# First head pair projected by seven products between the last gate/up chunks; row sums, down-weight sums, score pairs and final adds moved

## The chip, the cores and the metric

The kernel runs on one core of a Trainium2 chip. TensorE (PE) multiplies matrices into PSUM, VectorE (DVE), ScalarE (ACT) and GpSimd (POOL) work element by element, SyncE (SP) issues the transfers. Each engine works its own queue in order and waits on semaphores. The metric is the device time of one execution in microseconds; lower is better.

## The reference

```python
def _A_ref(x, k_cache, v_cache, wq, wo):            # H = 32 heads, Dh = 128, 2048 rows, D = 512
    q = transpose((x @ wq).reshape(B, Sq, H, Dh))
    scores = einsum("bhqd,bhkd->bhqk", q, k_cache) * (Dh ** -0.5)
    p = softmax(scores)
    return transpose(einsum("bhqk,bhkd->bhqd", p, v_cache)).reshape(B, Sq, H * Dh) @ wo

def _B_ref(x, W_gate, W_up, W_down):                # F = 1792
    gate, up = x @ W_gate, x @ W_up
    return (gate * (gate > 0) * up) @ W_down

xn = layernorm(x)
out = x + _A_ref(xn, k_cache, v_cache, wq, wo) * silu(_B_ref(xn, W_gate, W_up, W_down))
```

All inputs are bf16.

## The kernel before, in words

**Rows and blocks.** The 2048 rows are four blocks Q = 0 to 3 of 512 rows. A *chunk* is 128 of the 1792 gate/up columns (14 chunks, `fc`). Attention runs over 128 blocks b = (head h, Q), each of eight *key pairs* p (two times 128 keys). For a key pair TensorE makes two score matmuls (L1258), ScalarE one exponential of 128x1024 (L1270), and three pairs later (`LAG = 3`) TensorE makes eight P·V matmuls (L1367). At a block's end VectorE normalizes (L1287, L1290), and a transfer transposes the result into `OT_store`.

**Seven products.** Where four products of half-sized blocks would make a matrix product, this kernel often makes seven (Strassen's scheme as Winograd arranged it), from sums of the operands prepared ahead: `TX` (sums of the normalized rows, `emit_tx`), `SW` (sums of a head pair's Q weights, `emit_sw`), `SG` (gate/up weights, `gu_sums`), `WdT`/`Wd16` (down weights, `emit_wd_sums`), `HS_sb` (sums of h, `emit_hs`). `emit_st(pr, c, step)` makes the projection of head pair `pr` for the row halves c and c + 2 in four steps (products 1 and 2; 6 and 5; 7 and 3; 4) and combines them on VectorE with the accumulators `cu`, `cv`. `emit_d(Q, step)` does the same for the down projection of 512 rows; step 1 needs the seventh sum of h (`hs_tok[(Q, 1, 2)]`). Only pair 0 is projected plainly, by `emit_qp`: four matmuls for each head and row block.

**The PSUM ring.** Six banks `ps_r` are three slots of two banks. `ring_acquire` hands them out in turn, and TensorE waits there until the slot's former content was read. A gate/up chunk takes one, a score pair takes one, and `emit_M` puts extra work (a step of `emit_st`, `emit_d`, `emit_os`, two final tiles) into one.

**Order of the work.** The head centres the first 512 rows and runs their gate/up and down projection on TensorE; meanwhile VectorE computes the layer norm's statistics in `ln_task(i)`, one call for each chunk, GpSimd applies them (L409), and SP transposes the rows into `xnT` (L521). The first 512 rows are normalized last, and their transposes stand on SP's queue behind `issue_first` (the first K, Q-weight, V and output-weight loads) and in front of `gu_load(0)` and `gu_load(1)`. Then `emit_gate_up(2)` runs 14 chunks for Q = 2 (L656, L660); behind its chunks VectorE makes the down-weight scale (chunks 0, 1) and sums (2 to 5), the first half of the row sums (6 to 9) and half of the sums of h (10, 11), and ScalarE and GpSimd prepare two chunks of gate/up weights (`gu_sums`, behind chunks 4 and 6). After it come the plain projections of head 0 and three score pairs, and then the main loop. Its extra work is laid down by block and key pair: `plan` holds what goes into ring slots (`at(b, p, ...)`), `side` holds VectorE work put behind it, and `defer(n, ...)` postpones by n key pairs. In the main loop an iteration emits the score pair three ahead, its plan items, its side items, its deferred work, and the P·V of its own pair. The gate/up rows Q = 1 and 3 run by seven products inside blocks 2 to 13.

**The tail.** `emit_base` scales a 128-row tile of the accumulated result and adds the input (L1235, L1240; `base_at`), where `LB` is block 124. `emit_final_tile(n)` multiplies the last four heads' part (L1401); VectorE scales it by the gate into `fin_tmp` (L1409), GpSimd adds it to the base (L1425; VectorE for the last tile), and SP stores it (L1430).

The lines around the start of the main loop read:

```python
        for Q in range(0, QB, 2):
            emit_M([(emit_qp, 1, 0, Q), (emit_qp, 1, 0, Q + 1)])
        sp_head_start(0)
        for gp in range(LAG):
            open_S_pair(gp)
            emit_S_tile(gp, 0)
            emit_S_tile(gp, 1)
        emit_sw(1)
```

Of the kernel before, what the change touches and what calls it, by code (L numbers as in the profile page):

```python
# [52 lines left out]
def bass_recurrent_scan__mha_block_cached__glu_gated_reglu__prompt_kernel(  # L53
# [30 lines left out]
    LAG = 3  # L84
# [31 lines left out]
    with ExitStack() as es:  # L116
# [70 lines left out]
        cu = at_(92160, [128, NQ], F32, "cu")  # L187
        cv = at_(94208, [128, NQ], F32, "cv")
# [336 lines left out]
        def ln_task(i):  # L525
            if i < 4 * (QB - 1):
                ln_hold["st"] = ln_stats(4 + i)
                if i % 4 == 3:
                    ns = list(range(i + 1, i + 5))
                    ln_hold["sq"] = (ns, ln_sqrt(ns, ln_aggr(ns, ln_hold["st"])))  # L530
                elif i >= 4 and i % 4 == 0:
                    ln_finish(i // 4)
            elif i == 4 * (QB - 1):
                ln_finish(QB - 1)
                issue_first()
                ns = list(range(4))
                ln_hold["sq"] = (ns, ln_sqrt(ns, sem_ln2.cur()))
            elif i == 4 * (QB - 1) + 1:
                ctok = ln_finish(0)
                _wait(dve, ctok)  # L540
                rtok = sem_ln3.sig(
                    dve.scalar_tensor_tensor(r2[:], rstd[:, 0:4, :], YSC, rstd[:, 0:4, :],
                                             op0=ALU.mult, op1=ALU.mult))
                _wait(dve, rtok)
                ln_hold["r2"] = sem_ln3.sig(
                    dve.tensor_scalar(r2h[:], r2[:], 0.5 / YSC, None, op0=ALU.mult))
# [38 lines left out]
        def gu_sums(k):  # L585
# [13 lines left out]
            gu_tok[(k, "x")] = sem_sg.sig(pool.tensor_tensor(X[:, 3], a12, X[:, 1], ALU.subtract))  # L599

# [84 lines left out]
        def emit_wd_sums(k):  # L685
            DH = D // 2
            b11, b12 = Wd_sb[:, 0:HF, 0:DH], Wd_sb[:, 0:HF, DH:D]
            b21, b22 = Wd_sb[:, HF:FC, 0:DH], Wd_sb[:, HF:FC, DH:D]
            if k == 0:
                _wait_all(dve, [wd_tok[0], wd_tok[1], sem_nm.cur()])  # L690
            elif k != 2:
                _wait(dve, wd_tok["k"])
            if k == 0:
                t = dve.tensor_tensor(WdT[:, 0], b12, b11, ALU.subtract)
            elif k == 1:
                t = dve.tensor_tensor(WdT[:, 1], b22, WdT[:, 0], ALU.subtract)
            elif k == 2:
                t = dve.tensor_tensor(Wd16[:, 0:HF, DH:D], b22, b12, ALU.subtract)
            else:
                t = dve.tensor_tensor(WdT[:, 2], WdT[:, 1], b21, ALU.subtract)  # L700
            t = sem_wdt.sig(t)
            if k != 2:
                wd_tok["k"] = t
            wd_tok["t"] = t
# [68 lines left out]
        _wait(sp, sem_g.cur())  # L773
        gu_load(0)
        gu_load(1)
        hlast = emit_gate_up(2)

        qt_ready = {}
        qp_done_tok = {}
# [28 lines left out]
        def emit_qp(h, Q, bank):  # L808
            qs = slice(Q * NQ, (Q + 1) * NQ)
            _wait(pe, wq_tok(0))  # L810
            if h == 0 and Q == 0:
                _wait_all(pe, xt_ready[0])
            ins = None
            for c in range(DC):
                ins = pe.matmul(ps_r[:, bank, :], Wq_sb[0][:, c, h, :], xnT[:, c, qs],  # L815
                                start=(c == 0), stop=(c == DC - 1))
            qtok = sem_qp.sig(ins)
            if h == 1 and Q == QB - 1:
                qp_done_tok[0] = qtok
            dst = qt_take(h, Q)  # L820
            if h == 0 and Q % 2 == 1:
                _wait(act, qtok)
                etok = sem_gua.sig(act.copy(dst, ps_r[:, bank, :]))
            else:
                _wait(dve, qtok)
                etok = sem_qpe.sig(dve.tensor_copy(dst, ps_r[:, bank, :]))
            qt_ready[(h, Q)] = etok
            return etok

        sw_tok = {}  # L830

        def emit_sw(pr):
            b = pr % 2
            W = Wq_sb[b]
            _wait(pool, wq_tok(pr))
            if pr >= 3:
                _wait(pool, qp_done_tok[pr - 2])
            wflat = W[:].rearrange("p c i e -> p (c i e)")
            if pr == 2:
                _wait(act, wq_tok(pr))  # L840
                k = sem_w2s.sig(act.activation(wflat, wflat, ACTF.Copy, scale=WSC))
            else:
                k = sem_sw.sig(pool.tensor_scalar(wflat, wflat, WSC, None, op0=ALU.mult))  # L843
            sw_tok[(pr, 0)] = k
            _wait(pool, k)
            a11, a12 = W[:, 0:HC, 0, :], W[:, HC:DC, 0, :]
            a21, a22 = W[:, 0:HC, 1, :], W[:, HC:DC, 1, :]
            X = SW[b]
            if pr == 1:
                _wait(pool, glu_done_tok)  # L850
            k1 = sem_sw.sig(pool.tensor_tensor(X[:, 0], a21, a22, ALU.add))
            sem_sw.sig(pool.tensor_tensor(X[:, 2], a11, a21, ALU.subtract))
            _wait(pool, k1)
            k2 = sem_sw.sig(pool.tensor_tensor(X[:, 1], X[:, 0], a11, ALU.subtract))
            _wait(pool, k2)
            sw_tok[(pr, 1)] = sem_sw.sig(pool.tensor_tensor(X[:, 3], a12, X[:, 1], ALU.subtract))

        st_tok = {}

        def emit_st(pr, c, step, *banks):  # L860
            W, X = Wq_sb[pr % 2], SW[pr % 2]
# [120 lines left out]
        def emit_d(Q, step, *banks):  # L982
# [271 lines left out]
        def emit_S_tile(gp, tt):  # L1254
# [8 lines left out]
            if p == NP - 1:  # L1263
                qt_free.append((qt_slot[(h, Q)], stok))
                if Q == QB - 1:
# [5 lines left out]
                               scale=scale if h < 2 else scale / WSC)  # L1271
# [119 lines left out]
        def emit_final_tile(n, bank):  # L1391
# [12 lines left out]
            fb = fin_cnt[0] % NFT  # L1404
            fin_cnt[0] += 1
            _wait(dve, otok)
            _wait(dve, fin_free[fb])
            mtok = sem_opa.sig(
                dve.scalar_tensor_tensor(fin_tmp[fb], ps_r[:, bank, 0:D], 1.0 / (OSC * YSC), g_sb[:, n, :],  # L1409
                                         op0=ALU.mult, op1=ALU.mult))  # L1410
            fin_pending.append((n, fb, mtok))
            flush_final_add()
            return mtok

        fin_pending = []

        def flush_final_add():
            if not fin_pending:
                return
            n, fb, mtok = fin_pending.pop()  # L1420
            Q, j = divmod(n, 4)
            eng, sem = (dve, sem_opa) if n == NT - 1 else (pool, sem_hp)
            _wait(eng, mtok)
            _wait(eng, base_done[n])
            ftok = sem.sig(eng.tensor_tensor(g_sb[:, n, :], s_acc[:, n, :], fin_tmp[fb], ALU.add))  # L1425
            fin_free[fb] = ftok
            if Q == QB - 1 or j % 2 == 1:
                n0 = n if Q == QB - 1 else n - 1
                _wait(sp, ftok)
                sem_out.sig(sp.dma_start(out_t[:, n0:n + 1, :], g_sb[:, n0:n + 1, :]))  # L1430

# [5 lines left out]
        at(0, 0, (emit_qp, 1, 1, 0), (emit_qp, 1, 1, 1))  # L1437
        at(1, 0, (emit_qp, 1, 1, 2), (emit_qp, 1, 1, 3))
# [22 lines left out]
        dplan = {2: ((0, 2), (0, 5), (1, 2), (1, 5)),  # L1461
# [36 lines left out]
        base_at += [(LB + 1, 6), (LB + 1, 7), (LB + 2, 2), (LB + 2, 6)]  # L1498
# [7 lines left out]

        glu_done_tok = hlast
# [65 lines left out]
        flush_final_add()  # L1573
# [29 lines left out]
```

## Time and profile before

| | us |
|---|---|
| median of 3 runs | 1256.17 |
| lowest and highest | 1255.91, 1256.29 |
| the profiled execution: time | 1255.73 |
| the profiled execution: span of its instructions | 1254.1 |
| ScalarE's exponentials (1024 of them), busy | 969.9 |
| P·V matmuls, busy | 749.2 |
| score matmuls, busy | 652.7 |

The profile is that of one execution. A row of a timeline reads: start in us from the span's start, duration, engine, line, operation, output<-inputs, tile sizes, count, and in brackets the idle time before it and what ended it. "PE" is a matmul, "PEld" a weight load, "SPq" an issue on SyncE's queue. Consecutive instructions of one form are merged into a row. The recorded end of a matmul lies about 0.17 behind the start of the next, so durations of matmuls are read from start to start.

### The profile page before, as it was taken

What the parts mean: (1) busy time and instruction counts of PE and PEld (TensorE: products, weight loads), DVE (VectorE), ACT (ScalarE), POOL (GpSimd) and SP (SyncE); (2) the same over time, 40 slices, a digit from 0 to 9 for tenths busy, and PEclk for the clock granted to TensorE, in tenths of its full rate; (3) what the DMA queues carried; (4) which work ended last, traced back from release to release, by engine and by line L of the source; (5) the groups of instructions that cost most, each with busy time, mean ns of one, the idle gap of its engine ahead of it and who ended that gap; (6) DMA issues with size and microseconds to landing.
All of it is one profiled execution on the core that took longest, in us unless ns stands there. A gap on an engine that the chain in (4) does not pass through costs nothing.

```text
span 1254.1 us, 28671 instructions
## 1 busy us (share of the span) xinstructions
PE 1234.5 (98%) x12173; PEld 868.8 (69%) x12399; DVE 681.7 (54%) x1157; ACT 1020.3 (81%) x1108; POOL 290.3 (23%) x261
## 2 busy tenths in 40 slices
PE   9999999999999999999999999999999999999998
PEld 5466565777777777777777777777777777777774
DVE  6667777665444545454543544454544444446766
ACT  4357877668888888888888888888888888888894
POOL 2323999510401040100401040102200040100005
PEclk9999999999999999999999999999999999999999
DMA  9712431332223332443222232433333222343212
GB/s 273 155 31 31 78 79 27 51 48 34 48 44 56 69 60 47 60 68 56 52 41 44 57 56 52 60 64 60 51 56 68 50 34 42 60 81 68 67 33 76
DMA packets 250687, 78.02 MB, mean 62 GB/s; under 512 B 226241, under 2 KB 250561, under 8 KB 250561
## 3 DMA queue, kind: packets, MB, share of 16 engines
q1 hardware_dynamic: 249888, 75.79, 32.6%
q8 instruction: 98, 1.61, 0.6%
q10 hardware_dynamic: 672, 0.39, 0.1%
q14 instruction: 29, 0.23, 0.1%
HBM read 38.54 MB, written 2.10 MB: 32 GB/s over the span
## 4 chain that ended last, share of the span: by engine, by line
PE 84%; ACT 10%; POOL 2%; issue 1%; SPq 1%; DVE 1%; DMA 0%; POOLq 0%; DVEq 0%; ACTq 0%
PE ps_acc L1367 34%; PE ps_r L1258 28%; ACT PT L1270 10%; PE ps_r L1139 6%; PE ps_r L879 6%; PE ps_r L943 3%; PE ps_r L1002 3%; PE ps_r L656 1%; PE ps_r L660 1%; PE ps_r L1401 1%; PE ps_r L815 1%; POOL hT L921 0%; SPq L521 0%; POOL xn_sb L409 0%; POOL gB L919 0%
## 5 line engine op out<-in xcount | busy, mean ns | idle before, releaser
L1270 ACT ACTIVATE PT<-ps_r 128x1024 bf16<-128x1024 f32 x1024 | 969.9, 1028 | 161.2 <-PE ps_r L1258 149.7
L1367 PE MATMUL ps_acc<-V_sb,PT 128*128 128x129 bf16 x8192 | 749.2, 220 | 10.0 <-DVE Onorm L1290 1.3
L1367 PEld LDWEIGHTS ps_acc<-V_sb,PT 128*128 128x128 bf16 x8192 | 605.0, 98 | 219.0 <-ACT PT L1270 16.0
L1258 PE MATMUL ps_r<-QT_sb,KT_sb 128*128 128x512 bf16 x1831 | 652.7, 379 | 2.0 <-ACT PT L1270 0.2
L1157 DVE TENSOR_TENSOR s_acc<-s_acc,ps_r 128x512 f32<-128x512 f32 x264 | 167.7, 683 | 178.1 <-PE ps_r L1139 178.1
L843 POOL TENSOR_SCALAR Wq_sb<-Wq_sb 128x1024 bf16<-128x1024 bf16 x14 | 38.8, 2771 | 675.9 <-DMA Wq_sb<-in_A_wq_dram 675.9
L1258 PEld LDWEIGHTS ps_r<-QT_sb,KT_sb 128*128 128x128 bf16 x2048 | 188.0, 98 | 1.6 <-ACT PT L1270 0.7
L1287 DVE RECIPROCAL rz_sb<-ps_acc 128x4 f32<-128x4 f32 x127 | 23.2, 183 | 204.1 <-PE ps_acc L1367 203.8
L1290 DVE TENSOR_TENSOR Onorm<-ps_acc,rz_sb 128x512 bf16<-128x512 f32 x127 | 87.8, 691 | 4.4
L884 DVE TENSOR_TENSOR QT_sb<-cu,ps_r 128x512 bf16<-128x512 f32 x60 | 41.3, 688 | 84.6 <-PE ps_r L1258 79.5
L1425 POOL TENSOR_TENSOR g_sb<-s_acc,WX 128x512 bf16<-128x512 f32 x15 | 17.8, 1216 | 153.9 <-DVE WX L1409 153.9
L879 PE MATMUL ps_r<-xn_sb,SW 128*128 128x512 f16 x180 | 48.6, 379 | 0.0
L1139 PE MATMUL ps_r<-WX,OX 128*128 128x256 f16 x336 | 45.8, 273 | 0.0
L884 DVE TENSOR_TENSOR cu<-cu,ps_r 128x512 f32<-128x512 f32 x60 | 41.3, 688 | 0.0
L1139 PEld LDWEIGHTS ps_r<-WX,OX 128*128 128x128 f16 x336 | 32.9, 98 | 9.8 <-ACT PT L1270 0.2
L884 DVE TENSOR_TENSOR QT_sb<-cv,ps_r 128x512 bf16<-128x512 f32 x60 | 38.3, 680 | 0.0
L1081 POOL TENSOR_SCALAR Wo_sb<-Wo_sb 128x2048 bf16<-128x2048 bf16 x7 | 37.6, 5366 | 0.6
L879 PEld LDWEIGHTS ps_r<-xn_sb,SW 128*128 128x128 f16 x180 | 17.6, 98 | 21.3 <-ACT PT L1270 0.3
L879 PE MATMUL ps_r<-xnT,Wq_sb 128*128 128x512 bf16 x120 | 30.8, 379 | 0.0
L1139 PE MATMUL ps_r<-Wo_sb,OT_store 128*128 128x256 bf16 x224 | 29.0, 273 | 0.4
L616 ACT ACTIVATE gr_sb<-ps_r 128x512 bf16<-128x512 f32 x27 | 15.7, 593 | 16.7 <-PE ps_r L656 16.0
L919 POOL TENSOR_SCALAR gB<-gB 128x512 bf16<-128x512 bf16 x14 | 20.8, 1487 | 32.2 <-DVE gB L949 32.2
(151 smaller groups left out, 942.4 us busy)
## 6 DMA issues: line engine op xcount, KB each, us to landing
V_sb<-in_A_v_cache_dram SPq DMA_DIRECT2D x32, 512.0 KB, 4.8
Wq_sb<-in_A_wq_dram SPq DMA_DIRECT2D x16, 256.0 KB, 3.8
Wo_sb<-in_A_wo_dram SPq DMA_DIRECT2D x8, 512.0 KB, 3.8
xr_sb<-in_A_x_dram SPq DMA_DIRECT2D x16, 128.0 KB, 2.1
OT_store<-Onorm SPq DMA_TRANSPOSE x127, 2.5
Wd_sb<-in_B_W_down_dram SPq DMA_DIRECT2D x1, 1792.0 KB, 14.0
W<-in_B_W_gate_dram SPq DMA_DIRECT2D x14, 128.0 KB, 2.5
W<-in_B_W_up_dram SPq DMA_DIRECT2D x14, 128.0 KB, 2.8
```

The source lines that it names most:

```text
L843: k = sem_sw.sig(pool.tensor_scalar(wflat, wflat, WSC, None, op0=ALU.mult))
L879: ins = pe.matmul(ps_r[:, bank, :], L(i), R(i), start=(i == 0), stop=(i == HC - 1))
L884: return sem_qpe.sig(dve.tensor_tensor(dst, a, ps_r[:, bank, :], op))
L943: ins = pe.matmul(ps_r[:, bank, :], L(i), R(i), start=(i == 0), stop=(i == HC - 1))
L1002: ins = pe.matmul(ps_r[:, bank, j * DH:(j + 1) * DH], L(i), R(i), start=(i == 0 and j == 0), stop=(i == HF - 1 and j == 1))
L1081: k = sem_wx.sig(pool.tensor_scalar(wflat, wflat, WOSC, None, op0=ALU.mult))
L1139: ins = pe.matmul(ps_r[:, bank, j * DH:(j + 1) * DH], L(i), R(i), start=(i == 0 and j == 0), stop=(i == GH - 1 and j == 1))
L1157: t = dve.tensor_tensor(names[k], names[k], view(bank), op)
L1258: ins = pe.matmul(ps_r[:, 2 * s + tt, :], KT_sb[h % 2][:, t * 128:(t + 1) * 128], QT_sb[qt_slot[(h, Q)]][:], start=True, stop=True)
L1270: act.activation(PT[pb][:], ps_r[:, 2 * s:2 * s + 2, :], ACTF.Exp, scale=scale if h < 2 else scale / WSC)
L1290: dve.tensor_tensor(Onorm[ob][:], o_ap, rz_sb[:].to_broadcast([128, 4, Dh]), ALU.mult))
L1367: ins = pe.matmul(o_ap, PT[pb][:, tt, j * 128:(j + 1) * 128], V_sb[vb][:, t, 0:VW], start=(t == 0 and j % 2 == 0), stop=(t == KT - 1 and j ...
```

## The change

Pair 0 is projected by `emit_st` like the others; `emit_qp` is gone, and the exponential of heads 0 and 1 has the scale of the other heads. Pair 0's weight sums `SW0` and the accumulators `cuv0` of its first half lie in memory that the first `hT0` has left. Its first half and the first step of its second half run between the gate/up chunks 9 to 13, and the three first score pairs among them; the other three steps run in blocks 0 and 1. All eight row sums are made behind chunks 0 to 3, for which the first 512 rows are normalized first in the head. The down-weight scale goes behind chunks 4 and 5, the down-weight sums go to GpSimd behind chunk 5, `gu_sums` behind chunks 7 and 9, all sums of h into the key pairs 0 to 3 of block 0, the first down step from pair 2 to pair 0 of block 0. In the tail, VectorE makes the final adds of the tiles 0 to 7, 12 and 15, reading the scaled product from PSUM, and the last four base tiles move from block 125 (two) and block 126 (two) to other pairs of the blocks 126 and 127.

```diff
+        cuv0 = [at_(10240 - 2048 * i, [128, NQ], F32, "cuv0") for i in range(2)]
+        SW0 = at_(12288, [128, 4, DC // 2, Dh], F16, "SW0")
+        cuv = [at_(92160 + 2048 * i, [128, NQ], F32, "cuv") for i in range(2)]
...
         def ln_task(i):
             if i < 4 * (QB - 1):
+                if i == 1:
+                    ns = list(range(4))
+                    ln_hold["sq"] = (ns, ln_sqrt(ns, sem_ln2.cur()))
                 ln_hold["st"] = ln_stats(4 + i)
+                if i == 2:
+                    ctok = ln_finish(0)
...
                 ln_finish(QB - 1)
                 issue_first()
-                ns = list(range(4))
-                ln_hold["sq"] = (ns, ln_sqrt(ns, sem_ln2.cur()))
-            elif i == 4 * (QB - 1) + 1:
-                ctok = ln_finish(0)
...
+        def emit_sw(pr):
...
+            if pr == 0:
+                _wait(pool, tx_tok[(1, 3)])
...
+            if pr in (0, 2):
+                _wait(act, wq_tok(pr))
+                k = sem_w2s.sig(act.activation(wflat, wflat, ACTF.Copy, scale=WSC))
...
                 if Q == 2:
-                    if fc < 2:
-                        emit_wd_scale(fc)
+                    if fc < 4:
+                        emit_tx(2 * fc)
+                        emit_tx(2 * fc + 1)
                     elif fc < 6:
-                        emit_wd_sums(fc - 2)
-                    elif fc < 10:
-                        emit_tx(fc - 2)
-                    elif fc < 12:
-                        emit_hs(2, 0, 2 * (fc - 10))
-                        emit_hs(2, 0, 2 * (fc - 10) + 1)
-                    if fc in (4, 6):
-                        gu_sums(fc // 2 - 2)
+                        emit_wd_scale(fc - 4)
+                    if fc == 3:
+                        emit_sw(0)
+                    if fc == 5:
+                        for k in range(4):
+                            emit_wd_sums(k)
+                    if fc in (7, 9):
+                        gu_sums((fc - 7) // 2)
+                    if 9 <= fc < 12:
+                        emit_M([(emit_st, 2, 0, 0, fc - 9)])
+                    elif fc == 12:
+                        emit_S_pair(0)
+                        emit_M([(emit_st, 1, 0, 0, 3)])
+                    elif fc == 13:
+                        emit_S_pair(1)
+                        emit_M([(emit_st, 2, 0, 1, 0)])
+                        emit_S_pair(2)
...
-                t = dve.tensor_tensor(WdT[:, 0], b12, b11, ALU.subtract)
+                t = pool.tensor_tensor(WdT[:, 0], b12, b11, ALU.subtract)
...
             if step == 0:
                 _wait(pe, h_done[(Q, FC - 1)])
                 if Q == 2:
-                    _wait_all(pe, [wd_tok[0], wd_tok[1], wd_tok["t"]])
+                    _wait_all(pe, [wd_tok[0], wd_tok[1]])
...
             if step == 1:
                 _wait(pe, hs_tok[(Q, 1, 2)])
+                _wait(pe, wd_tok["t"])
...
+            sums_on_dve = n < NT - 8 or n in (NT - 4, NT - 1)
...
+            if sums_on_dve:
+                mtok = ftok = sem.sig(eng.tensor_tensor(g_sb[:, n, :], prod, s_acc[:, n, :], ALU.add))
+            else:
+                ftok = fin_free[fb] = sem.sig(eng.tensor_tensor(g_sb[:, n, :], s_acc[:, n, :], prod, ALU.add))
...
-        at(0, 0, (emit_qp, 1, 1, 0), (emit_qp, 1, 1, 1))
-        at(1, 0, (emit_qp, 1, 1, 2), (emit_qp, 1, 1, 3))
+        for step, b, p in ((1, 0, 3), (2, 1, 0), (3, 1, 3)):
+            at(b, p, (emit_st, 1 if step == 3 else 2, 0, 1, step))
...
-        dplan = {2: ((0, 2), (0, 5), (1, 2), (1, 5)),
+        dplan = {2: ((0, 0), (0, 5), (1, 2), (1, 5)),
...
-        hs_at = {2: [(1, i, 0, i) for i in range(4)]}
+        hs_at = {2: [(k // 4, k % 4, 0, k // 2) for k in range(8)]}
...
-        for i in range(4):
-            side.setdefault((i // 2, (6, 7)[i % 2] if i < 2 else (1, 3)[i % 2]), []).append((emit_tx, i))
...
-        base_at += [(LB + 1, 6), (LB + 1, 7), (LB + 2, 2), (LB + 2, 6)]
+        base_at += [(LB + 2, 2), (LB + 2, 5), (LB + 3, 1), (LB + 3, 3)]
...
-        for Q in range(0, QB, 2):
-            emit_M([(emit_qp, 1, 0, Q), (emit_qp, 1, 0, Q + 1)])
         sp_head_start(0)
-        for gp in range(LAG):
-            open_S_pair(gp)
-            emit_S_tile(gp, 0)
-            emit_S_tile(gp, 1)
         emit_sw(1)
```

More of the change, by code (lines that the diff above doesn't have):

```diff
@@ L806, in qt_take @@
             return QT_sb[i][:]
[L808 to L856, printed above, removed]
         st_tok = {}
         def emit_st(pr, c, step, *banks):
-            W, X = Wq_sb[pr % 2], SW[pr % 2]
+            W, X = Wq_sb[pr % 2], SW[pr % 2] if pr else SW0
+            cu, cv = cuv0 if pr == 0 and c == 0 else cuv
             lo = slice(c * NQ, (c + 1) * NQ)
@@ L887, in emit_st @@
                 _wait(pe, sw_tok[(pr, 0)])
+                if pr == 0 and c == 0:
+                    _wait_all(pe, xt_ready[0])
                 p1 = prod(1, banks[0])
@@ L1270, in emit_S_tile @@
                 act.activation(PT[pb][:], ps_r[:, 2 * s:2 * s + 2, :], ACTF.Exp,
-                               scale=scale if h < 2 else scale / WSC)
+                               scale=scale / WSC)
             )
@@ L1505, in bass_recurrent_scan__mha_block_cached__glu_gated_reglu__prompt_kernel, with emit_S_pair @@
                 plan[(LB + 2 + Q, 4 * (j // 2))][-1].append((emit_final_tile, 1, 4 * Q + j))
+        def emit_S_pair(gp):
+            open_S_pair(gp)
+            emit_S_tile(gp, 0)
+            emit_S_tile(gp, 1)
+        assert LAG == 3 and FC == 14
+        _wait(sp, sem_g.cur())
+        gu_load(0)
+        gu_load(1)
+        hlast = emit_gate_up(2)
         glu_done_tok = hlast
@@ L1572, in bass_recurrent_scan__mha_block_cached__glu_gated_reglu__prompt_kernel @@
             emit_M([(emit_final_tile, 1, n), (emit_final_tile, 1, n + 1)])
-        flush_final_add()
         sp.wait_ge(sem_out.h, sem_out.n)
```

84 lines of the change are left out of this document (48 added, 36 removed).

## The prediction

> **What bounds the kernel now.** I read the page first: engine totals, granted clock, the chain that ended last.
>
> ```profile
> PE 1234.5 (98%) x12173; PEld 868.8 (69%) x12399; DVE 681.7 (54%) x1157; ACT 1020.3 (81%) x1108; POOL 290.3 (23%) x261
> PEclk9999999999999999999999999999999999999999
> PE 84%; ACT 10%; POOL 2%; issue 1%; SPq 1%; DVE 1%; DMA 0%; POOLq 0%; DVEq 0%; ACTq 0%
> ```
>
> TensorE is busy 98% of the span at full clock and carries 84% of the chain, so a microsecond that TensorE does not compute or wait is a microsecond of the result. The question is where TensorE waits. I therefore read its timeline over the stretch that the change rebuilds, from the first gate/up chunk of Q=2 to pair 1's first projection.
>
> ```profile
> 43.33 1.03 PE L656 MATMUL ps_r<-xnT,Wg_sb 128*128 128x512 bf16 x4
> 46.18 5.40 SPq L521 DMA_TRANSPOSE xnT<-xn_sb  x4
> 55.17 1.06 ACT L589 ACTIVATE W<-W 128x1024 bf16<-128x1024 bf16 x1 [3.27 <-DMA W<-in_B_W_up_dram]
> 55.41 1.03 PE L656 MATMUL ps_r<-xnT,Wg_sb 128*128 128x512 bf16 x4
> 57.65 1.02 PE L656 MATMUL ps_r<-xnT,Wg_sb 128*128 128x512 bf16 x4 [0.34 <-DVE hT L620]
> ...
> 68.00 3.79 PE L815 MATMUL ps_r<-xnT,Wq_sb 128*128 128x512 bf16 x16
> 71.63 1.52 PE L1258 MATMUL ps_r<-QT_sb,KT_sb 128*128 128x512 bf16 x6
> 73.40 0.61 PE L1258 MATMUL ps_r<-QT_sb,KT_sb 128*128 128x512 bf16 x2 [0.25 <-ACT PT L1270]
> 74.31 1.90 PE L815 MATMUL ps_r<-xnT,Wq_sb 128*128 128x512 bf16 x8 [0.31 <-ACT PT L1270]
> 76.05 1.06 PE L1367 MATMUL ps_acc<-V_sb,PT 128*128 128x129 bf16 x12
> 77.82 3.22 PE L1002 MATMUL ps_r<-Wd_sb,hT 128*128 128x256 bf16 x28
> 80.88 0.62 PE L1367 MATMUL ps_acc<-V_sb,PT 128*128 128x129 bf16 x8
> 81.33 0.38 PE L1258 MATMUL ps_r<-QT_sb,KT_sb 128*128 128x512 bf16 x1
> 83.53 1.69 PE L1002 MATMUL ps_r<-WdT,HS_sb 128*128 128x256 f16 x14
> 102.64 1.03 PE L879 MATMUL ps_r<-xnT,Wq_sb 128*128 128x512 bf16 x4
> ```
>
> Starts give prices: from 43.33 to 55.41 are seven chunks, 1.726 each, so a 512-column matmul takes 0.216; 28 down matmuls take 3.06 (77.82 to 80.88); one P·V of a key pair takes 0.45 (80.88 to 81.33); one key-pair step is 0.45 + 2 x 0.216 = 0.88. From 43.33 to 102.64 are 59.31 us. The work in them: 112 gate/up, 32 projection and 40 score matmuls (184 x 0.216 = 39.7), 98 down matmuls (10.7), 16 P·V (7.2), together 57.65. So TensorE waits 1.65 there. Of these, 0.5 lie before 57.65 (the chunk of 55.41 should have been followed at 57.14): the weights of the later gate/up rows are loaded only behind four transposes of 5.40, ScalarE waits 3.27 for them and is late with a relu. The rest lies between 71.6 and 76.05, where nothing but six score matmuls is ready while the first exponentials run.
>
> **The change, part by part.** *Seven products.* 32 projection matmuls become 28: -0.86.
>
> *The two waits.* The normalization of the first 512 rows moves to the front of the head, so their four transposes leave the place ahead of the weight loads, and the weights are asked for after the chunks 7 and 9 instead of 4 and 6: the 0.5 goes. In the head VectorE gets about 1.3 us of small instructions behind its third chunk; it needs the ring only three chunks later (5.2 us), so I cost them at nothing. The score pairs now run between chunks 12, 13 and the loop, and the exponentials beside them: the 1.15 goes. Together -1.65.
>
> *New small waits.* I laid out TensorE's new order, each unit taking the slot used three units before. Chunk 9 starts at 43.33 + 9 x 1.726 = 58.87. TensorE is ready for chunk 13 at 69.3, but its slot was chunk 12's, whose product comes on VectorE behind the three combinations of product step 2 (from 66.6, four times 0.65, and 0.2 of delay: 69.5), so 0.2. It is ready for the first down step at 73.4; that slot was the projection step's of 71.7 to 72.5, whose copy and dependent combination (0.79 + 0.69, prices below) run from 72.3 to 73.8: 0.4. Together +0.65 with rounding. The first down step then ends at 76.9 (58.87 + five chunks 8.63 + 18 projection and 8 score matmuls 5.61 + waits 0.65 + 3.06 = 76.8).
>
> *Row sums and scales on VectorE in chunks 0 to 5.* Eight sums and two scales come to the six hT products.
>
> ```profile
> 59.07 0.68 DVE L562 TENSOR_TENSOR xn_sb<-xnT 128x1024 f16<-128x1024 bf16 x1
> 45.97 1.08 DVE L683 TENSOR_SCALAR Wd_sb<-Wd_sb 128x3584 bf16<-128x3584 bf16 x1
> ```
>
> 8 x 0.6 + 2 x 1.05 + 6 x 0.6 = 10.5 us in six chunks of 10.4: VectorE stays about one chunk behind, two are allowed. Nothing. If the sums were blocked as below, a chunk would wait at most about a microsecond.
>
> *The sums of h, all in block 0.* This is where I expect the price. Four of the eight leave the end of gate/up and stand, two for each key pair, in pairs 0 to 3 of block 0, on VectorE behind the first down step's last combination; the second down step (pair 5) waits for the seventh of them, and in front of that one stand also the gating product and the two combinations of the moved projection step.
>
> ```profile
> 65.87 0.69 DVE L718 TENSOR_TENSOR HS_sb<-hT 128x1024 f16<-128x1024 f16 x1
> 66.59 0.69 DVE L721 TENSOR_TENSOR hT<-hT 128x1024 f16<-128x1024 f16 x1
> 67.20 0.68 DVE L620 TENSOR_TENSOR hT<-gr_sb,ps_r 128x512 f16<-128x512 bf16 x1
> ...
> 76.86 0.55 DVE L718 TENSOR_TENSOR HS_sb<-hT 128x768 f16<-128x768 f16 x1
> 77.44 0.56 DVE L721 TENSOR_TENSOR hT<-hT 128x768 f16<-128x768 f16 x1
> 82.27 0.56 DVE L727 TENSOR_TENSOR HS_sb<-hT,HS_sb 128x768 f16<-128x768 f16 x1
> 82.75 0.68 DVE L1024 SCALAR_TENSOR_TENSOR g_sb<-dbuf,dbuf 128x512 bf16<-128x512 f32 x1
> ...
> 103.27 0.69 DVE L891 COPY cu<-ps_r 128x512 f32<-128x512 f32 x1
> 104.06 0.69 DVE L884 TENSOR_TENSOR QT_sb<-cu,ps_r 128x512 bf16<-128x512 f32 x1
> ```
>
> A dependent sum follows after 0.72, a free one after 0.6; the shorter ones after 0.58 and 0.48; a dependent combination after 0.79. VectorE's queue from the end of the first down step (76.9 + 0.2): combination 0.61, three sums 2.16, a fourth 0.60, two short ones 0.58 + 0.48, gating 0.60, two combinations 0.79 + 0.60, the seventh sum 0.55: 7.0, done at 84.1. TensorE meanwhile has P·V 0.45, pairs 1 and 2 (1.77), pair 3 with its projection step (1.75), pair 4 (0.88), two scores (0.43): 5.3, ready at 82.2. So it waits 1.9 even if nothing disturbs VectorE. In the kernel before the sums were done at 82.8 and the step began at 83.53: there they had 0.7 to spare.
>
> *Down-weight sums on GpSimd.* They take GpSimd's time, and GpSimd disturbs VectorE.
>
> ```profile
> L921 POOL TENSOR_TENSOR hT<-gB,uB 128x512 f16<-128x512 bf16 x14 | 16.2, 1157 | 1.2
> 60.24 0.66 POOL L594 TENSOR_TENSOR SG<-W 128x256 f16<-128x256 bf16 x1
> 60.27 1.18 DVE L564 TENSOR_TENSOR xn_sb<-xnT 128x1024 f16<-128x1024 bf16 x1
> 63.66 2.77 POOL L843 TENSOR_SCALAR Wq_sb<-Wq_sb 128x1024 bf16<-128x1024 bf16 x1
> ```
>
> 256 elements take 0.66, 512 take 1.157, so 1792 take 1.157 + 5 x 0.49 = 3.6, and the four 14.4 us. GpSimd begins with pair 0's sums when the row sums end (about 53) and with the down-weight sums at 56 to 58; it ends them at 70 to 72, the gate/up sums (8 x 0.66) at 76 to 78, pair 1's scale (2.77) at 78 to 80, pair 1's four sums at 81 to 83. The down-weight sums themselves are wanted only at 82: hidden. But what stands behind them now falls on 76 to 83, on top of the sums of h. The rows of 60.24 and 60.27 show such a meeting: the VectorE sum that began beside a GpSimd one took 1.18 for 0.68, half a microsecond more. The row of 63.66 overlaps the undisturbed sum of 65.87, so the scale blocks at most its first part. Four to six meetings at 0.5 to 0.6 are 2 to 3.5; I take 3.1. The wait becomes 5.0; its ends are 0 (the order of VectorE is kinder than I read it) and 8 (below).
>
> [...]
>
> *The tail.* The last four base tiles leave block 125.
>
> ```profile
> 1221.85 1.89 PE L1401 MATMUL ps_r<-Wo_sb,OT_store 128*128 128x512 bf16 x8
> 1223.94 0.18 DVE L1287 RECIPROCAL rz_sb<-ps_acc 128x4 f32<-128x4 f32 x1
> 1224.99 0.61 PE L1367 MATMUL ps_acc<-V_sb,PT 128*128 128x129 bf16 x8 [1.25 <-DVE Onorm L1290]
> 1243.85 0.17 DVE L1310 RECIPROCAL rz_sb<-ps_acc 128x2 f32<-128x2 f32 x1
> 1246.16 5.60 POOL L1425 TENSOR_TENSOR g_sb<-s_acc,WX 128x512 bf16<-128x512 f32 x5 [0.77 <-DVE WX L1409]
> 1250.66 1.65 DVE L1425 TENSOR_TENSOR g_sb<-s_acc,WX 128x512 bf16<-128x512 f32 x1
> 1251.79 0.88 SPq L1430 DMA_DIRECT2D out_dram<-g_sb  x2
> ```
>
> TensorE's eight matmuls end at 1223.58, the next start at 1224.99: 1.41 lost, because VectorE normalizes only at 1223.94, behind base tiles. That goes: -1.41. Against it, VectorE now also adds tiles 0 to 7 (8 x 0.7); four such instructions for tiles 6 and 7 (2.8 from 1238.7 on in the shifted time) and the products of tiles 8 and 9 (1.2) end at about 1242.9, where the reciprocal of 1243.85, shifted by 1.41, would stand at 1242.4: about 0.45 late. At the end the adds of tiles 13 and 14 stay on GpSimd (5.60 / 5 = 1.12 each) and their stores ahead of the last on SP's queue, so of the last VectorE add's 1.65 only about 0.14 is won. Together -1.1.
>
> **Sum:** -0.86 - 1.65 + 0.65 + 5.0 - 1.1 = +2.0. The profiled execution took 1255.73 (span 1254.1), 0.44 under the median of 1256.17; 1257.8 on its scale, 1258.2 on the median's. I forecast 1258.2.
>
> **Rivals.** *The queue alone:* GpSimd is done, or not yet at pair 1's sums, when the sums of h run. The wait is 1.9, the sum -1.1: 1255.1. For it: GpSimd's end is known to no better than 3 us. Against it: it has 25 us of work queued from 57, and the sums of h start at 77.7.
>
> *No wait at the second down step:* all else as above, -3.0: 1253.2. For it: VectorE is idle for half of these microseconds before. Against it: 7.0 against 5.3 in rows that hardly vary.
>
> *The lock as the bound (slower):* if the down-weight sums still run when the sums of h begin, each meeting lasts up to 3.6 and the second down step waits for the weight sums too. It decides from an end of the weight sums later than 77.7, which needs 5.2 each instead of 3.6; the wait is then 7 to 9, the sum +4 to +6: 1260 to 1262. For it: 1792 elements are extrapolated from 512. Against it: between 57 and 71 VectorE has only work with an operand in PSUM, with nothing for GpSimd to meet. [...]
>
> **How the numbers follow.** Chances: the forecast 0.42 (its own range 1257.2 to 1259.7, waits of 4.0 to 6.5), the queue alone 0.16, no wait 0.23, the lock 0.19. A difference of 0.2%, 2.5 us, is about what a measurement of this kernel can tell from no change: the bounds are 1253.7 and 1258.7. Faster: two thirds of "no wait", 0.16. Slower: 0.18 of the lock and 0.4 of the forecast's 0.42, 0.36. The rest, 0.48, is the same. The range 1253.0 to 1261.0 takes in both ends of the wait but the outermost of either.
>
> **What would show it.** Right: chunks without a gap up to 12; first exponential near 69; second down step at 84 or later, with TensorE idle before it and VectorE's L718 to L727 rows there over 1 us; the 1.25 wait of block 126 gone. Wrong: second down step at 82.2 (no wait), or down-weight sums ending after 77 (the lock). A gap in chunks 3 to 9 would mean that the row sums are not covered.

## The result and the profile after

The changed kernel takes 1257.83 us (median of 18 runs, 1257.27 to 1259.08), the kernel before 1255.84 us on the same chip (18 runs, 1255.42 to 1256.42): a ratio of 1.0017, 95% interval 1.0009 to 1.0024. The forecast was 1258.2. The profiled execution of the changed kernel took 1257.72 (span 1256.4, against 1254.1 before). In the experiments below one run of E1 (7505 us, the only one profiled, so that E1 is read by its times) and one of the kernel before (3385 us, beside E9) are left out.

TensorE's timeline of the changed kernel (start, busy time, instruction, idle time ahead and its releaser), from the first down step of Q=2 to pair 1's first projection:

```profile
68.84 0.59 PE L868 MATMUL ps_r<-xn_sb,Wq_sb 128*128 128x512 f16 x2
69.44 1.02 PE L689 MATMUL ps_r<-xnT,Wg_sb 128*128 128x512 bf16 x4
...
73.77 3.23 PE L993 MATMUL ps_r<-Wd_sb,hT 128*128 128x256 bf16 x28 [0.28 <-DVE QT_sb L873]
...
81.69 0.59 PE L1250 MATMUL ps_r<-QT_sb,KT_sb 128*128 128x512 bf16 x2
86.20 2.05 PE L993 MATMUL ps_r<-WdT,HS_sb 128*128 128x256 f16 x14 [3.91 <-DVE cuv L873]
88.04 3.04 PE L993 MATMUL ps_r<-WdT,hT 128*128 128x256 f16 x14
90.92 0.62 PE L1359 MATMUL ps_acc<-V_sb,PT 128*128 128x129 bf16 x8
...
106.54 1.03 PE L868 MATMUL ps_r<-xnT,Wq_sb 128*128 128x512 bf16 x4
```

The first down step starts at 73.77 instead of 77.82: that part came as planned. Two 512-column matmuls from 81.69 take 0.43, so TensorE is ready at 82.12 for the second down step and starts it at 86.20: a wait of 4.08 (the row's 3.91 is shorter since ends are modelled; starts are the safer reading). The step, 28 matmuls, then takes 4.72 (86.20 to 90.92) where the same count took 3.06 before. Pair 1's projection, at 102.64 before, starts at 106.54.

Why the same matmuls take longer shows in the stretches of this kernel (bounds, length, busy time and count of TensorE, weight loads, VectorE, ScalarE and GpSimd, then granted clock, DMA share and GB/s):

```profile
84.00:86.00 2.00, 0.00 (x0) 0.00 (x0) 1.90 (x3) 0.00 (x0) 1.92 (x4) 1.00 0.00 0
...
87.00:88.00 1.00, 1.00 (x9) 0.81 (x7) 0.04 (x1) 0.00 (x0) 0.00 (x0) 0.69 0.00 0
88.00:90.00 2.00, 2.00 (x12) 1.40 (x10) 0.69 (x1) 0.00 (x0) 0.00 (x0) 0.50 0.00 0
90.00:92.00 2.00, 2.00 (x20) 1.54 (x19) 0.69 (x1) 0.00 (x0) 0.00 (x0) 0.80 0.00 0
```

In 84 to 86 TensorE does nothing, at a granted clock of 1.00. From about 87.4 (the 0.31 lost in 87 to 88 are 0.62 us at one half) to about 90.8 the granted clock is one half: it falls only some 1.2 us after the step has begun. The lost shares, 0.31 + 2 x 0.50 + 2 x 0.20 = 1.71, match the 1.66 that the step takes longer. The page's clock line, forty slices of 31 us, shows nothing of it.

VectorE's rows in front of that step, in the changed kernel:

```profile
77.64 0.78 DVE L761 TENSOR_TENSOR HS_sb<-hT 128x1024 f16<-128x1024 f16 x1
78.45 0.69 DVE L764 TENSOR_TENSOR hT<-hT 128x1024 f16<-128x1024 f16 x1
79.18 0.69 DVE L767 TENSOR_TENSOR HS_sb<-hT 128x1024 f16<-128x1024 f16 x1
79.91 1.04 DVE L770 TENSOR_TENSOR HS_sb<-hT,HS_sb 128x1024 f16<-128x1024 f16 x1
80.87 1.02 DVE L761 TENSOR_TENSOR HS_sb<-hT 128x768 f16<-128x768 f16 x1
81.92 0.91 DVE L764 TENSOR_TENSOR hT<-hT 128x768 f16<-128x768 f16 x1
82.76 1.15 DVE L1015 SCALAR_TENSOR_TENSOR g_sb<-dbuf,dbuf 128x512 bf16<-128x512 f32 x1
83.83 1.46 DVE L873 TENSOR_TENSOR cuv<-cuv,ps_r 128x512 f32<-128x512 f32 x2
85.21 0.89 DVE L767 TENSOR_TENSOR HS_sb<-hT 128x768 f16<-128x768 f16 x1
```

And GpSimd's beside them:

```profile
68.03 3.58 POOL L743 TENSOR_TENSOR WdT<-WdT,Wd_sb 128x1792 f16<-128x1792 f16 x1
...
76.84 2.77 POOL L619 TENSOR_SCALAR Wq_sb<-Wq_sb 128x1024 bf16<-128x1024 bf16 x1
79.69 0.71 POOL L627 TENSOR_TENSOR SW<-Wq_sb 128x256 f16<-128x256 bf16 x1
80.36 1.11 POOL L628 TENSOR_TENSOR SW<-Wq_sb 128x256 f16<-128x256 bf16 x1
81.44 0.98 POOL L630 TENSOR_TENSOR SW<-SW,Wq_sb 128x256 f16<-128x256 f16 x1
82.50 0.86 POOL L632 TENSOR_TENSOR SW<-Wq_sb,SW 128x256 f16<-128x256 bf16 x1
...
85.03 0.66 POOL L599 TENSOR_TENSOR SG<-SG,W 128x256 f16<-128x256 f16 x1
```

The seventh sum of h ends at 85.21 + 0.89 = 86.10, and the step follows 0.10 later; the releaser named in TensorE's row (`cuv`, 83.83 + 1.46) had long been done, so it is the sum. Each two-input VectorE row from 79.91 on, with all operands in SBUF, is 0.34 to 0.47 longer than the same form elsewhere (0.69, 0.55, 0.56, 0.68); the three rows beside GpSimd's 2.77 us scale are not, but for 0.09 on the first. The two combinations at 83.83 (one operand in PSUM) take 1.46 together, and 1.47 in E3, where GpSimd does nothing beside them. GpSimd's sums of 256 elements grow as well, from 0.67 to up to 1.11.

In the tail, TensorE's rows of the changed kernel:

```profile
1225.71 1.89 PE L1394 MATMUL ps_r<-Wo_sb,OT_store 128*128 128x512 bf16 x8
1227.43 0.62 PE L1359 MATMUL ps_acc<-V_sb,PT 128*128 128x129 bf16 x8
...
1247.64 0.39 PE L1331 MATMUL ps_r<-ident,Onorm 128*128 128x128 bf16 x4
```

and the last of these in the kernel before:

```profile
1245.19 0.39 PE L1339 MATMUL ps_r<-ident,Onorm 128*128 128x128 bf16 x4
```

P·V of block 126 follows its eight matmuls without a gap: 1227.43 is 2.44 after the 1224.99 of before, where the tail began 3.86 late (1225.71 against 1221.85), so 1.42 is won. The transposes at 1247.64 are 2.45 late: nothing is lost again until there. The span ends 2.3 late, so 0.14 more is won at the end.

### The profile page after: what moved, and what is told of

The parts are those of the page before. It is cut to its first block, busy times and chain, and to the rows that moved or that the text cites. A ratio compares the mean times of both kernels' runs of the same rounds, so it can differ in the third digit from the quotient of the medians.

```text
span 1256.4 us, 28900 instructions
## 1 busy us (share of the span) xinstructions
PE 1246.8 (99%) x12395; PEld 869.6 (69%) x12395; DVE 686.7 (55%) x1172; ACT 1020.3 (81%) x1107; POOL 296.5 (24%) x260
## 4 chain that ended last, share of the span: by engine, by line
PE 88%; issue 8%; POOL 2%; DVE 1%; DMA 0%; ACT 0%; POOLq 0%; DVEq 0%
PE ps_acc L1359 33%; PE ps_r L1250 31%; PE ps_r L868 7%; PE ps_r L1131 6%; PE ps_r L934 3%; PE ps_r L993 3%; PE ps_r L689 2%; PE ps_r L693 2%; PE ps_acc L790 1%; POOL g_sb L1414 0%; POOL hT L912 0%; POOL gB L910 0%; POOL gA L910 0%; DMA x_sb<-in_A_x_dram 0%; PE ps_r L506 0%
## 5 line engine op out<-in xcount | busy, mean ns | idle before, releaser
L1250 PE MATMUL ps_r<-QT_sb,KT_sb 128*128 128x512 bf16 x2048 | 726.7, 379 | 0.0
L873 DVE TENSOR_TENSOR QT_sb<-cuv,ps_r 128x512 bf16<-128x512 f32 x128 | 84.9, 684 | 85.6 <-PE ps_r L1250 79.5
L873 DVE TENSOR_TENSOR cuv<-cuv,ps_r 128x512 f32<-128x512 f32 x96 | 65.9, 687 | 3.3
L868 PE MATMUL ps_r<-xn_sb,SW 128*128 128x512 f16 x192 | 51.9, 379 | 0.0
L1414 POOL TENSOR_TENSOR g_sb<-s_acc,WX 128x512 bf16<-128x512 f32 x6 | 6.8, 1154 | 162.9 <-DVE WX L1407 162.9
L1131 PEld LDWEIGHTS ps_r<-Wo_sb,OT_store 128*128 128x128 bf16 x224 | 21.9, 98 | 8.5
```

The costliest lines, as they stand in the source:

```text
L868: ins = pe.matmul(ps_r[:, bank, :], L(i), R(i), start=(i == 0), stop=(i == HC - 1))
L873: return sem_qpe.sig(dve.tensor_tensor(dst, a, ps_r[:, bank, :], op))
L1131: ins = pe.matmul(ps_r[:, bank, j * DH:(j + 1) * DH], L(i), R(i), start=(i == 0 and j == 0), stop=(i == GH - 1 and j == 1))
L1250: ins = pe.matmul(ps_r[:, 2 * s + tt, :], KT_sb[h % 2][:, t * 128:(t + 1) * 128], QT_sb[qt_slot[(h, Q)]][:], start=True, stop=True)
```

## The experiments

All were timed in five rounds beside the kernel before, whose medians were 1256.09 (E1 to E4), 1256.14 (E5 to E8) and 1255.69 (E9). The changed kernel's 18 runs stood beside 1255.84. These medians of one and the same kernel differ by up to 0.45, so medians of kernels that were timed beside different ones are not compared more finely than that.

### E1: the tail alone

The kernel before, with the changed kernel's final tiles and the last four base tiles moved:

```diff
-base_at += [(LB + 1, 6), (LB + 1, 7), (LB + 2, 2), (LB + 2, 6)]
+base_at += [(LB + 2, 2), (LB + 2, 5), (LB + 3, 1), (LB + 3, 3)]
...
+sums_on_dve = n < NT - 8 or n in (NT - 4, NT - 1)
```

> The kernel before with the edits of the tail alone (final adds of tiles 0 to 7, 12 and 15 on VectorE, last four base tiles later). My theory: these edits act alone, and the profile of the changed kernel shows 1.42 us won at block 126 and 0.14 at the end; so 1.5 us under the kernel before, 1254.3, and TensorE's 1.25 wait in front of block 126's P*V is gone. Rival: in the changed kernel the tail only looks shorter because it comes later against the stores and GpSimd; then 0 to 0.5 us under the kernel before.

Measured: 1254.25 us, ratio 0.9985 (0.9976 to 0.9994): -1.8. The tail is a gain of its own, near the -1.56 read from the trace.

### E2: the wait filled with work

The changed kernel, with 17 score matmuls written to a slot that is overwritten behind them, so that the wait stays and TensorE does not idle in it:

```diff
 open_S_pair(gp)
+if (bq, pq) == (0, 5):
+    for _i in range(17):
+        pe.matmul(ps_r[:, 2 * s_slot[gp], :], KT_sb[0][:, 0:128],
+                  QT_sb[qt_slot[(h, Q)]][:], start=True, stop=True)
 emit_S_tile(gp, 0)
```

> The changed kernel with 17 needless 512-column matmuls (3.7 us) in the slot of the score pair of block 0, pair 5, in front of its real ones, so that TensorE works in most of its 4.08 us wait; nothing that the second down step waits for moves. My theory: the step's 4.72 us instead of 3.06 come from the granted clock, which the idle time halved for 3.41 us; so the step takes 3.06 again, the clock stays 1.00, and the time falls by 1.66 us to about 1256.2, with less scatter. Rival: the step is slow because of its operands or because GpSimd and VectorE work beside it; then the step still takes over 4 us and the time does not fall.

Measured: 1256.04 us, ratio 1.0001 (0.9992 to 1.0010), and a spread of 0.4 instead of 1.8. TensorE's timeline of this kernel:

```profile
81.64 3.83 PE L1522 MATMUL ps_r<-QT_sb,KT_sb 128*128 128x512 bf16 x16
...
86.14 1.69 PE L993 MATMUL ps_r<-WdT,HS_sb 128*128 128x256 f16 x14 [0.25 <-issue]
...
89.20 0.62 PE L1359 MATMUL ps_acc<-V_sb,PT 128*128 128x129 bf16 x8
```

(One of the 17 is missing from the records.) The step starts where it did (86.14), but takes 3.06 instead of 4.72. Useless matmuls make the kernel 1.79 us faster by the two medians, 2.04 by the differences to the kernel before beside each: the slow half of the step is the price of idling before it, not of the step's operands.

### E3: GpSimd held back

Pair 1's scale and sums and the third block of gate/up sums wait for the eighth sum of h:

```diff
 sp_head_start(0)
-emit_sw(1)
...
 if pq == 4 and bq == 0:
+    _wait(pool, hs_tok[(2, 1, 3)])
     gu_sums(2)
+    emit_sw(1)
```

> The changed kernel with GpSimd's work for pair 1 and for the third gate/up chunk held until VectorE has ended its sums of h, so that nothing of GpSimd meets them. My theory: the meetings cost 2.1 of the 4.08 us; the seventh sum ends at about 84.1 and the wait is 1.9 to 2.0 us, too short for the clock to fall; time 2.1 + 1.66 = 3.8 us under the changed kernel, 1254.0. Rival A (VectorE's queue is long by itself, the meetings cost nothing): wait 4 us, same time. Rival B (the clock falls after 2 us of idling as well): 1255.7.

Measured: 1254.02 us, ratio 0.9985 (0.9976 to 0.9993). VectorE's rows of this kernel:

```profile
79.72 0.69 DVE L770 TENSOR_TENSOR HS_sb<-hT,HS_sb 128x1024 f16<-128x1024 f16 x1
...
83.39 0.55 DVE L767 TENSOR_TENSOR HS_sb<-hT 128x768 f16<-128x768 f16 x1
```

and TensorE's:

```profile
81.61 0.59 PE L1250 MATMUL ps_r<-QT_sb,KT_sb 128*128 128x512 bf16 x2
84.04 1.69 PE L993 MATMUL ps_r<-WdT,HS_sb 128*128 128x256 f16 x14 [1.84 <-DVE cuv L873]
```

The sums are back at their undisturbed lengths; the wait is 84.04 - 82.04 = 2.00 instead of 4.08, and the clock stays at full: 1.00 in every stretch read from 80 to 100 (the step's first half is 1.69 where it was 2.05). So 2.08 us of the wait were meetings with GpSimd. The difference to E2, whose clock is 1.00 from 80 to 100 too, says the same in medians: 1256.04 - 1254.02 = 2.02.

### E4: the sums first as well

E3, with the seventh and eighth sum in pair 2 of block 0 and the projection step behind the second down step:

```diff
-hs_at = {2: [(k // 4, k % 4, 0, k // 2) for k in range(8)]}
+hs_at = {2: [(k // 4, k % 4, 0, min(k // 2, 2)) for k in range(8)]}
...
-for step, b, p in ((1, 0, 3), (2, 1, 0), (3, 1, 3)):
+for step, b, p in ((1, 0, 6), (2, 1, 0), (3, 1, 3)):
```

> As the run before, and VectorE's queue set in another order: the last two sums of h in pair 2 instead of 3, the third projection step from pair 3 to pair 6, so that the seventh sum stands behind six sums alone. My theory: it ends at about 82.1, TensorE is ready at 82.1 minus 0.9 for the moved step, 81.3, so the wait is about 0.8; all of the 5.7 us but that go: 5 us under the changed kernel, about 1252.8, which beats both. Rival (the wait is only moved: to the moved step, the third down step or the norm of block 0): 1254 or more, with an idle TensorE shown elsewhere between 82 and 105.

Measured: 1252.99 us, ratio 0.9977 (0.9968 to 0.9986): the best of all kernels here, 3.1 us under the kernel before. TensorE's rows of this kernel:

```profile
80.80 0.59 PE L1250 MATMUL ps_r<-QT_sb,KT_sb 128*128 128x512 bf16 x2
82.23 1.69 PE L993 MATMUL ps_r<-WdT,HS_sb 128*128 128x256 f16 x14 [0.83 <-issue]
```

Ready at 81.23, started at 82.23, behind a seventh sum that ends at 82.13: of the wait 1.00 is left. The order on VectorE was worth the other 1.0.

### E5: the first sums back beside the long GpSimd sums

The changed kernel, with the first four sums of h behind chunks 10 and 11, where they stood before the change:

```diff
+if fc in (10, 11):
+    emit_hs(2, 0, 2 * (fc - 10))
+    emit_hs(2, 0, 2 * (fc - 10) + 1)
...
-hs_at = {2: [(k // 4, k % 4, 0, k // 2) for k in range(8)]}
+hs_at = {2: [(1, i, 0, i // 2) for i in range(4)]}
```

> Changed kernel, but the four sums of the first half of h of Q=2 stand where they stood before the change: two behind chunk 10, two behind chunk 11, so beside GpSimd's down-weight sums (3.58 us each). Theory (a VectorE sum waits for the whole of a GpSimd sum that is running): the L761 to L770 rows of those chunks are mostly 2 us and longer, the hT products behind them come late and TensorE loses 2 to 6 us in chunks 12 to the first down step; the second down step no longer waits and the clock stays at full (-5.7): 1254 to 1258. Rival (a meeting costs about 0.4 us, as the rows of 1.04 against 0.69 suggest, however long the GpSimd instruction is): rows of about 1.1, nothing lost in the chunks, 1252.1.

Measured: a median of 1259.87 us, ratio 1.0031 (1.0021 to 1.0041), with 4 of 8 runs at 1259.07 to 1259.25 and 4 at 1260.49 to 1261.84. The profiled run is of the second group. Two VectorE rows of this kernel and the GpSimd rows that ran with them:

```profile
65.08 3.94 DVE L767 TENSOR_TENSOR hT<-hT 128x1024 f16<-128x1024 f16 x1
...
70.93 2.08 DVE L770 TENSOR_TENSOR HS_sb<-hT 128x1024 f16<-128x1024 f16 x1
```

```profile
64.45 4.03 POOL L744 TENSOR_TENSOR Wd<-Wd_sb 128x1792 f16<-128x1792 bf16 x1
68.44 4.02 POOL L746 TENSOR_TENSOR WdT<-WdT,Wd_sb 128x1792 f16<-128x1792 f16 x1
```

A sum of 0.69 took 3.94: it was issued at 65.08 and ended at 69.02, just behind the GpSimd sum's 68.48; the next one ended at 73.01, behind 72.46. So in these two rows VectorE waited until the running GpSimd instruction of 4.03 or 4.02 had ended, not for a fixed 0.4. TensorE's rows show what that cost there:

```profile
66.42 0.59 PE L871 MATMUL ps_r<-xnT,SW 128*128 128x512 bf16 x2
70.47 1.89 PE L689 MATMUL ps_r<-xnT,Wg_sb 128*128 128x512 bf16 x4 [3.46 <-DVE cuv L876]
72.15 1.91 PE L693 MATMUL ps_r<-xnT,Wu_sb 128*128 128x512 bf16 x4
```

It waited 3.6 (66.85 to 70.47), and then ran four matmuls in 1.7 instead of 0.86: the granted clock of its stretches was 0.56 in 69 to 73, 0.50 in 73 to 77 and 0.66 in 77 to 81. The lost shares, 4 x 0.44 + 4 x 0.50 + 4 x 0.34 = 5.1, are 10.2 us at one half, three times as long as in the changed kernel. The theory's mechanism shows in these two rows, its count (mostly rows over 2 us) and its range (1254 to 1258) do not hold: only two of the four sums were caught by the long instructions (a third, of 1.04, by a short one), and the slow clock came on top. The second down step follows its two score matmuls without a wait there (90.47 + 0.43 = 90.90), as the theory said. Not every long GpSimd instruction does this: the 2.77 us scale of the changed kernel, above, left the second and third sum beside it at 0.69.

### E6: the order alone

E4's order, with GpSimd where the change puts it (the diff of E4 alone, on the changed kernel).

> Only the order on VectorE is changed (seventh and eighth sum of h in pair 2 of block 0, projection step behind the second down step); GpSimd keeps its place, so its sums still run beside them. Theory (order and meetings both count): seventh sum done at about 83.7 instead of 82.1 in the kernel that holds GpSimd back, second down step at about 83.8, clock at full since the wait is only 2.5: 1254.5. Rival (only the order counts): 1253.0. Rival (only the meetings count): 1256 and a second down step at 85 or later.

Measured: a median of 1256.23 us, ratio 0.9996 (0.9988 to 1.0005), but in two groups: 3 of 11 runs at 1254.70 to 1254.75, 8 at 1256.08 to 1256.49. The profiled run, of the first group, has a granted clock of 1.00 from 80 to 92 and the step near where the first theory put it (83.8), 0.11 behind its seventh sum (82.99 + 0.90 = 83.89):

```profile
80.94 0.59 PE L1250 MATMUL ps_r<-QT_sb,KT_sb 128*128 128x512 bf16 x2
84.00 1.69 PE L993 MATMUL ps_r<-WdT,HS_sb 128*128 128x256 f16 x14 [2.47 <-ACT PT L1262]
```

In those runs the meetings cost 84.00 - 82.23 = 1.77 over E4, and 1254.7 - 1253.0 says the same. The theory that a wait of 2.5 is too short to cost clock does not hold for the other eight: no profile of them was taken, but their recorded mean clock is 0.998 to 0.999, and 1.000 in the three.

### E7: a wait of 3.2

E2 with 5 matmuls instead of 17.

> Changed kernel with 5 instead of 17 idle-filling score matmuls ahead of the second down step (1.08 us), so that TensorE still waits about 3.0 us for the seventh sum. Theory (the clock falls only behind a wait near 4 us): the granted clock stays at 1.0 and the time is that of the filled wait, 1256.1. Rival (any wait of some us halves the clock): 1257.8 with a second half of the step at 3 us.

Measured: a median of 1257.82 us, ratio 1.0008 (0.9999 to 1.0017), again in two groups: 3 of 11 runs at 1255.99 to 1256.15 (the theory's number), 8 at 1257.37 to 1258.20 (the rival's). The profiled run is of the second group:

```profile
83.24 0.38 PE L1250 MATMUL ps_r<-QT_sb,KT_sb 128*128 128x512 bf16 x1
86.67 3.14 PE L993 MATMUL ps_r<-WdT,HS_sb 128*128 128x256 f16 x14 [3.06 <-DVE cuv L873]
```

Here it is the step's first half that is slow (3.14, where it took 1.69 in E2), at a granted clock of 0.65 in 86 to 88 and 0.50 in 88 to 90. The mean clock sorts the runs as the times do: 1.000 in the three, 0.998 to 0.999 in the eight. Neither theory is right: the clock falls in some runs and not in others, and what decides it is not shown.

### E8: the step one pair later

E4 with the second down step in pair 6 and the projection step in pair 7:

```diff
-dplan = {2: ((0, 0), (0, 5), (1, 2), (1, 5)),
+dplan = {2: ((0, 0), (0, 6), (1, 2), (1, 5)),
```

> Best order so far (GpSimd held back, seventh and eighth sum of h first) with the second down step in pair 6 and the projection step in pair 7 of block 0. Theory: TensorE had 0.83 us left to wait at pair 5; one pair later is 0.88, so the wait goes: 1252.1. Rival (the 0.83 is not for the sums but for the step's own slot or start): it stays, 1253.0.

Measured: 1253.43 us, ratio 0.9977 (0.9967 to 0.9987); no better than E4. The step in TensorE's rows of this kernel:

```profile
83.09 1.70 PE L993 MATMUL ps_r<-WdT,HS_sb 128*128 128x256 f16 x14 [0.73 <-ACT PT L1262]
```

and ScalarE's before it:

```profile
81.06 1.07 ACT L591 ACTIVATE W<-W 128x1024 bf16<-128x1024 bf16 x1
82.00 2.87 ACT L1262 ACTIVATE PT<-ps_r 128x1024 bf16<-128x1024 f32 x3
```

The seventh sum is done at 82.21 there (VectorE, 81.65 + 0.56), yet the step starts at 83.09, behind an exponential. One exponential takes 1.03 in these rows, so the first of the three ends at about 83.0, and it began only behind L591, which scales the third block of gate/up weights for `gu_sums`. So the sum no longer bounds the step, and the rival, a wait for its slot, holds. Moved by one pair, the step meets another bound; whether that one goes when L591 stands elsewhere was not tried.

### E9: the front alone

The changed kernel with the final tiles and base tiles of before.

> Changed kernel with the tail of the kernel before (base tiles of blocks 126 and 127 and the adds of the last tiles as they were): the front alone. Theory (front +3.86 and tail -1.56 simply add): the wait of 1.25 at the first key pair of block 126 is back, pair 1's first projection is as late as in the changed kernel, 1257.8 + 1.56 = 1259.4, ratio about 1.0027. Rival (the tail's wait moves with the front or is partly absorbed, so that the parts don't add): 1258.4 or less.

Measured: 1259.48 us (7 runs), ratio 1.0032 (1.0021 to 1.0044). With E1 the parts add: -1.84 (E1) + 3.79 (E9) = +1.95, against +1.99 for the whole. The wait at block 126 is back in its trace (the last row below). One run, the profiled one, took 1257.67, the other six 1258.95 or more; its TensorE rows show it without the slow stretch:

```profile
86.25 1.69 PE L993 MATMUL ps_r<-WdT,HS_sb 128*128 128x256 f16 x14 [3.91 <-DVE cuv L873]
87.77 1.69 PE L993 MATMUL ps_r<-WdT,hT 128*128 128x256 f16 x14
...
104.92 1.03 PE L868 MATMUL ps_r<-xnT,Wq_sb 128*128 128x512 bf16 x4
...
1227.26 0.61 PE L1359 MATMUL ps_acc<-V_sb,PT 128*128 128x129 bf16 x8 [1.25 <-DVE Onorm L1282]
```

The same idle time of 3.91 before the step as in the changed kernel, and yet a granted clock of 1.00 from 82 to 92, both halves at 1.69 and pair 1's projection 1.62 earlier (104.92 against 106.54).

## Why the prediction was right, and where it was not

The total was right, a change of +2.0 against +1.99, and that it came so close was luck: three terms were off, by -1.0 (the meetings), +1.7 (the clock) and -0.5 (the tail), and nearly cancelled.

| term (us) | predicted | measured |
|---|---|---|
| front, without the wait at the second down step and the slower matmuls behind it | -1.86 | -1.9 |
| wait at that step, VectorE undisturbed | 1.9 | 2.00 (E3) |
| the wait's part from meetings with GpSimd | 3.1 | 2.08 (after against E3) |
| slower matmuls of the step | none | 1.66 (after; 1.79 by E2's median) |
| tail | -1.1 | -1.56 |
| sum | +2.0 | +2.3 in the span, +1.99 in the time |

The measured -1.9 is what is left of the front: 3.90 at pair 1's projection, less 0.04 by which the first chunk started later, less 4.08 and 1.66.

*The front's order.* The new small waits, 0.65 predicted, read 0.17 at chunk 13 (68.84 + 0.43 = 69.27 to 69.44) and 0.28 at the first down step, which began at 73.77 where the prediction had 73.8. There is no gap in chunks 3 to 12: the row sums on VectorE are covered, as costed. The first exponential starts at 69.04 ("near 69").

*The queue of the sums.* The mechanism was the predicted one, instruction by instruction, and E3 gives its undisturbed wait within 0.1. The rival "no wait" is out by the changed kernel's wait of 4.08 and by E3's of 2.00; the rival "the queue alone" is E3's kernel, which exists only if GpSimd is held back.

*The meetings.* "Four to six meetings at 0.5 to 0.6", taken as 3.1, was too large: there were five, of 0.34 to 0.47 (79.91, 80.87, 81.92, 82.76, 85.21), together 1.98, and 0.09 at the scale. Two of the four sums among them took over 1 us (1.04 and 1.02), as the sign of being right asked, the others 0.91 and 0.89. The rows show what a meeting is: each of the five ends 0.14 (to within 0.01) less than its own undisturbed length after the end of the GpSimd sum that was running when it began. For the seventh sum, 85.03 + 0.66 = 85.69, and 85.69 + 0.55 - 0.14 = 86.10. So in these rows VectorE waited for the rest of the running GpSimd instruction, and that rest was short here because those sums have only 256 elements (0.67 undisturbed). E5 shows the same with sums of 1792 elements (4.03 and 4.02 there, 3.58 undisturbed): its two rows end 0.54 and 0.55 after GpSimd's, which is 0.69 less 0.15 and 0.14.

*The lock as the bound.* It didn't occur, for the reason given against it: the down-weight sums took 3.58 (3.6 predicted), ended at 71.6 (70 to 72), and met no sum of h. Beside them VectorE's rows `hT<-gr_sb,ps_r` and `QT_sb<-cuv,ps_r`, with an operand in PSUM, took 0.69 each. That one meeting could last up to 3.6 was the author's estimate, from GpSimd's extrapolated length; in E5 two sums of 0.69 took 3.94 and 2.08, and the kernel a median of 1259.87.

*The clock.* This step of the prediction failed: it priced a wait at its length and the 28 matmuls behind it at 3.06, and had no term for the clock after an idle stretch. They took 4.72; E2 shows the missing 1.66 by itself.

*The tail.* The 1.41 at block 126 came (1.42), and 0.14 at the end. The 0.45 of lateness did not, because the wrong reciprocal was read. The first one, at 1243.85 before, stands at 1246.48, only 0.19 more than the 2.44 by which the whole stretch is late; the transposes wait for the second:

```profile
1246.97 0.17 DVE L1302 RECIPROCAL rz_sb<-ps_acc 128x2 f32<-128x2 f32 x1 [0.33 <-PE ps_acc L1359]
```

Before that one VectorE still stands idle for 0.33 (0.51 in the kernel before) until TensorE's last P·V.

*Small slips.* Of the last four base tiles two leave block 125, not four; the other two stood in block 126. By the prediction's own products the chances are 0.15 faster, 0.50 the same and 0.35 slower, where it has 0.16, 0.48 and 0.36.

## What to carry to other kernels

Price not only a wait of the bounding engine but the work behind it: here a wait of 4.08 us cost 5.7. Where VectorE and GpSimd both add tensors in SBUF, look at which instruction of the one stands beside which of the other and how long the other's is: sums of 0.69 took 1.04 beside a GpSimd instruction of 0.71, and 3.94 (E5) beside one of 4.03. Holding GpSimd's work back by 8 us, when nothing needed it sooner, was worth about 3.8 us. And a change of two independent halves should be timed in halves: this one's tail won 1.8 and its front lost 3.8, and the sum of 2 shows neither.

## What was not expected of the hardware

Around TensorE's wait of 4.08 the granted clock fell to one half for about 3.4 us in the profiled run of the changed kernel (1.71 of lost shares in the stretches above, divided by one half). In E5's it did for 10.2 us, around a wait of 3.6; a second wait, of 1.01 before 75.93, fell into the slow stretch. In the profiled run of E9 it stayed at 1.00 around the same wait of 4.08. What decides it, no run here shows. By the length of the wait, from the traces, and the groups of times:

| kernel | wait, us | runs with the longer time |
|---|---|---|
| E3 | 2.00 | 0 of 11 |
| E6 | 2.63 | 8 of 11 (+1.5) |
| E7 | 3.21 | 8 of 11 (+1.9) |
| after, E9 | 4.08 | 18 of 18, 6 of 7 (+1.2 or more) |

For E6, E7 and E9 a profile of one group stands above; the other group, and all of the changed kernel's runs but the profiled one, are sorted by their times. The mean clock sorts E6 and E7 alike, but 0.999 by itself proves nothing: 11 of the 33 runs of the kernel before beside E1 to E4 have it too. Five of the changed kernel's runs (1258.41 to 1259.08) and three of E9's (1260.07 to 1260.44) lie about 1 us above the rest at a lower mean clock, 0.996 to 0.997; no profile of such a run was taken, and whether the slow stretch is longer there, as in E5, stays open.
